# One key-tile sequence for batches three to seven of a sliding-window attention with an MLP behind it

## The chip, the cores and the metric

The kernel runs on one core of a Trainium2 chip. The metric is the device time of one launch in microseconds (us). PE is the matrix engine, ACT the scalar engine, DVE the vector engine, POOL GpSimd, and SP the sync engine, which here only issues DMAs. "L849" is line 849 of the kernel before.

## The reference, cut to what matters

```python
batch, n_heads, seq, head_dim = (8, 8, 576, 64)
window = 32
scores = (q @ k^T) / sqrt(64)
mask = abs(pos[:, None] - pos[None, :]) <= window
attn = softmax(where(mask, scores, -1e9))
x = (attn @ v) -> [4608 tokens, 512]      # 8 batches x 576 tokens, heads side by side
h = x @ w_in                               # w_in 512 x 2048
g = s * relu(h)^2 + b
out = g @ w_out                            # w_out 2048 x 512, float32
```

Each token attends to at most 65 tokens of its own batch and head. The MLP then runs over all 4608 tokens.

## The kernel before, in words

*Attention.* The 576 keys of a batch are cut into 9 tiles of 64 (NTILE). A tile of keys meets a window of 128 queries: its own 64 and 32 on either side. Two neighbouring tiles make a unit, on the two halves of the partitions, so a batch has 5 units (NUNIT), and the fifth has only one tile. A unit is one PE part for the scores (`qk_part`, L594, 64x64 corners of the array), an exponential on ACT (L620), a product with a 0/1 band mask on DVE (L624), a PE part for probabilities times V (`av_part`, L650), and `finish`: a reciprocal and a product on DVE (L670, L672), and then the transpose into XT, the MLP's input. In batches 0 to 2 that transpose is done by PE and copied by ACT (L679, L684), from batch 3 on by a DMA transpose from SP (L690). A unit's output are the 128 rows from 32 ahead of its first key; 96 in the first and the last unit of a batch. The V part of one unit and the score part of the next are issued together (`unit`, `pe_part`, LAG = 1).

*Loads.* q and k of batches 2 and up come in pieces (`piece`): one DMA for 512 rows, a cast to bf16 (L543, in two halves), a DMA transpose from SP (L550), and for k a reordering copy on POOL (L560). V comes by unit (`load_v`) and is cast on DVE (L485). `late(b)` says which engine issues these loads: SP for b < LATE, ACT from there on. Loads are held back by `paced`, which waits for an earlier unit's V part. q, k and V have two slots each, by the parity of the batch.

*MLP.* Tokens are cut into blocks of 96, 128, 288 and eight times 512. `s1` makes one 128-wide slice of h for a block (L849: 4 matmuls), ACT takes the relu (L856), DVE squares it (L858). `s2` sums 16 matmuls for 128 tokens into O (L867), DVE scales and shifts (L880), SP writes out. s1 of a block needs XT of all its tokens: block 4 (tokens 1024 to 1535) needs batch 2's rows.

*Order.* No order of instructions is written by hand. `_Graph` holds tasks with a cost, dependencies and a key (about when it is due); `plan` schedules them as a list, each engine taking the task that can start first, then the smaller key. It also models the two DMA queues (SP, ACT): each transfer has a size and a cost, RING bounds what stands in a queue before the issuing engine has to wait, and ACT only issues when its queue is short (CALM). Each engine then runs its list strictly in order. So a changed cost or key may change the order of anything.

Of the kernel before, what the change touches and what calls it, by code (L numbers as in the profile page):

```python
# [18 lines left out]
NUNIT = (NTILE + 1) // 2  # L19
VW = 66  # L20
# [9 lines left out]
XPE = 3  # L30
PACE = ((-1, -1, -1),) * 3
CASTS = 20.0
LATE = 2
AFTERV = 4
KTV = 0
CASTE = (("pool", "pool"), ("dve", "dve"))
# [24 lines left out]
class _Graph:  # L61
# [6 lines left out]
    RING, CALM, ISSUE, WRITE = 112.0, 40.0, 1400.0, 600.0  # L68
# [37 lines left out]
    def plan(self):  # L106
# [63 lines left out]
        while len(order) < len(self.tasks):  # L170
# [35 lines left out]
            room.clear()  # L206
        self.order = order
# [96 lines left out]
def bass_sliding_window_symmetric__then__act_starrelu_kernel(  # L304
# [22 lines left out]
    with ExitStack() as es:  # L327
# [24 lines left out]
        VB = [sb((128, NUNIT, H, VW), BF16, "vb") for _ in range(2)]  # L352
        EXS = sb((128, NEX, 2, NPAIR, 128), BF16, "ex")
        EX = [EXS[:, i, :, :, :] for i in range(NEX)]
        MASK = sb((128, 128), BF16, "mask")
# [43 lines left out]
        def unit_rows(m):  # L399
            lo = max(0, 128 * m - WIN)  # L400
            return lo, min(S, 128 * m + 128 - WIN)

        def due(b, m):
            tok = b * S + unit_rows(m)[0]
            blk = next(x for x in range(NM) if TBLK[x][0] + TBLK[x][1] > tok)
            f = (tok - TBLK[blk][0]) / TBLK[blk][1]
            before = PH[blk] - PH[blk - 1] if blk > 0 else 4.0
            return PH[blk] - 14.0 - (1.0 - f) * before
# [20 lines left out]
        for p0 in (0, 64):  # L429
            band(MASK[p0:p0 + 64, :], ONESW[p0:p0 + 64, :], ("MASK", p0), 0, 64, -96)  # L430
        for i in range(2):
            for c0 in (0, WIN + S):
                zero("dve", QT[i][:, :, c0:c0 + WIN], ("QTZ", i, c0), 150, key=-98 if i == 0 else -20)
            add("dve", lambda e, i=i: e.memset(VB[i].rearrange("p t h c -> p (t h) c")[:, :, D:D + 1], 1.0), 150,
# [13 lines left out]
        def load_weights(which, i, x, key, eng):  # L448
# [6 lines left out]
            else:  # L455
# [4 lines left out]
                dma=("l", 16, 92.0) if which == "in" else ("l", 32, 50.0))  # L460
# [5 lines left out]
        def paced(b, u):  # L466

            return land["av", b - 1, u] if u >= 0 else land["av", b - 2, NUNIT + u]

# [4 lines left out]
        def load_v(b, t, key, waits=()):  # L474

            n = min(128, S - 128 * t)
            add(late(b),
                lambda e: e.dma_start(VST[0:n, t, :, :], v[b, :, 128 * t:128 * t + n, :].rearrange("h p d -> p h d")),
                650.0, writes=[("VST", t)], key=key, dma=("l", n // 2, 23.0), waits=waits)
            land["v", b, t] = g.tasks[-1]  # L480

        def cast_v(b, t, key, eng, slack):
            slot, n = b % 2, min(128, S - 128 * t)
            add(eng, (lambda e: e.copy(VB[slot][0:n, t, :, 0:D], VST[0:n, t, :, :])) if eng == "act" else
                (lambda e: e.tensor_copy(VB[slot][0:n, t, :, 0:D], VST[0:n, t, :, :])),  # L485
                {"act": 617.0, "dve": 420.0, "pool": 750.0}[eng],
                reads=[("VST", t)], writes=[("V", slot, t)], key=key, slack=slack)

        def load_pair(b, name, pr, key, load_key, banks, eng, slack):
# [6 lines left out]
                600.0, writes=[("STG", si)], key=load_key, dma=("l", 8, 112.0))  # L496
# [26 lines left out]
        def piece(b, parts, key, waits):  # L523
# [16 lines left out]
                dma=("l", sum(n for _, _, n, _ in parts) // 8, 68.0))  # L540
# [26 lines left out]
        def later(b, key):  # L567
# [6 lines left out]
            for i, parts in enumerate(((("q", 0, 512, 0),), (("k", 0, 512, 0),), (("q", 512, 64, 0), ("k", 512, 64, 32)))):  # L574
                piece(b, parts, key + 0.01 * i, [paced(b, PACE[min(b, 4) - 2][i])] +
                      ([land["v", b - 1, AFTERV]] if b > (1 if LATE == 2 else 2) and AFTERV >= 0 else []))
# [8 lines left out]
        def buffers(b, u):  # L585
            n = b * NUNIT + u
            return EX[n % NEX], n % NEX, EX[(n - 1) % NEX], (n - 1) % NEX

        def tiles(u):
            return [j for j in (2 * u, 2 * u + 1) if j < NTILE]  # L590

        def qk_part(b, u, hps=(0, 1)):
            slot = b % 2
            fns = [lambda e, pr=pr, j=j, hp=hp: e.matmul(  # L594
                SC[64 * (j % 2):64 * (j % 2) + 64, hp, pr * 128:pr * 128 + 128],
                lhsT=KT[slot][64 * hp:64 * hp + 64, pr, 64 * j:64 * j + 64],
                rhs=q_window(b, pr, j)[64 * hp:64 * hp + 64], start=True, stop=True)
                for pr in range(NPAIR) for j in tiles(u) for hp in hps]
            lo, hi = max(0, 128 * u - WIN), min(S, 128 * u + 128 + WIN)
            reads = [("QT", slot, x, pr) for x in pieces(lo, hi, 64) for pr in range(NPAIR)]  # L600
            reads += [("KT", slot, x, pr) for x in tiles(u) for pr in range(NPAIR)]
            if u == 0:
                reads.append(("QTZ", slot, 0))
            if u == NUNIT - 1:
                reads.append(("QTZ", slot, WIN + S))
            return fns, reads, [("SC", hp) for hp in hps], 230.0 if len(hps) == 2 or u == NUNIT - 1 else 440.0

        def exp_mask(b, u, hps=((0, 1),)):
            key = due(b, u)
            ex, ei, _, _ = buffers(b, u)  # L610
            n = 64 * len(tiles(u))
            for hs in hps:
                dst, src = ex[0:n, hs[0]:hs[-1] + 1, :, :], SC[0:n, hs[0]:hs[-1] + 1, :].rearrange("p i (a c) -> p i a c", a=NPAIR)
                flat = dst.rearrange("p i a c -> p (i a) c")
                if b > 1:
                    flat_src = src.rearrange("p i a c -> p (i a) c").rearrange("p a (i c) -> p a c i", i=4)
                    flat_dst = flat.rearrange("p a (c i) -> p a c i", i=4)
                else:
# [4 lines left out]
                mask = MASK[0:n, :].rearrange("p (one c) -> p one c", one=1).to_broadcast((n, 4 * len(hs), 128))  # L623
                add("dve", lambda e, flat=flat, mask=mask: e.tensor_tensor(flat, flat, mask, ALU.mult),  # L624
                    130 + 0.53 * 512 * len(hs), reads=[("E", ei, hp, pr) for hp in hs for pr in range(NPAIR)] + [("MASK", p0) for p0 in (0, 64)],
# [6 lines left out]
        def av_part(b, u):  # L632


            slot = b % 2
            ex, ei, px, pi = buffers(b, u)
            bank, res = av_banks(b, u)
# [3 lines left out]
            def put(h, x, g):  # L641
# [3 lines left out]
                if not 0 <= j < NTILE:  # L645
# [7 lines left out]
                    rhs=VB[slot][64 * g:64 * g + 64, j // 2, h, 0:D + 1], start=first, stop=True,  # L653
# [339 lines left out]
```

The softmax here doesn't subtract the row's maximum and nothing guards it: scores larger than these inputs give would overflow.

## Time and profile before

| | |
|---|---|
| time, median of 3 runs | 324.03 us (323.0 to 324.18) |
| span in the profile | 321.4 us |
| PE, ACT, DVE, POOL busy | 295.8, 141.2, 206.6, 66.1 us |
| s1 matmuls (L849) and s2 matmuls (L867) | 139.6 and 139.6 us busy |
| exp of a unit (L620), 35 times | 1.02 us each, with 64 partitions as with 128 |
| mask product (L624), 35 times | 0.76 us each |
| reciprocal, product (L670, L672), 34 times each | 0.20 and 0.69 us each |
| cast of q/k pieces (L543) on DVE, POOL | 0.68, 1.04 to 1.38 us each |

Busy time of PE has overlaps and modelled ends, so idle time is better read from gaps and waits. The first score parts of batches 2, 3 and 4 begin at 80.89, 103.1 and 132.0 us; the last V part begins at 256.7 us. From there to the end there is MLP only.

### The profile page before, as it was taken

To read this page: it belongs to the slowest core of one execution; us is meant where nothing else is said; L and a number is where in the kernel's file an instruction comes from. 1 tells how busy PE (TensorE), PEld (TensorE's weight loads), DVE (VectorE), ACT (ScalarE), POOL (GpSimd) and SP (SyncE) were. 2 spreads that over 40 slices of the span, in tenths; PEclk is the share of its full clock that TensorE was granted. 3 is DMA by queue.
4 is the path that set the end of the run, shared out by engine and by line. 5 is a ranking of instruction groups with operands and counts; after the bars stand their busy time and mean duration, and the time that the engine had idled before them with its cause. 6 is when DMAs were issued, how large, how long until landed. Compare 5 with 4: busy or idle time off the path is not lost.

```text
span 321.4 us, 8084 instructions
## 1 busy us (share of the span) xinstructions
PE 295.8 (92%) x3410; PEld 160.8 (50%) x3452; DVE 206.6 (64%) x402; ACT 141.2 (44%) x219; POOL 66.1 (21%) x78
## 2 busy tenths in 40 slices
PE   2776999999998999999999999999999999999995
PEld 2564787755554444454444444454444444444442
DVE  2764678767869894979477769786965543333311
ACT  3653366445423863455055544553454423333200
POOL 3446454555106000600140006001500000000000
PEclk9999999999999999999999999999999999999999
DMA  7999999897995999789929994999312210000021
GB/s 254 292 284 332 355 209 335 289 230 186 214 234 175 280 151 181 172 244 190 229 90 306 146 223 85 294 187 224 93 49 67 69 60 33 35 33 33 35 98 66
DMA packets 104580, 56.70 MB, mean 176 GB/s; under 512 B 77216, under 2 KB 96160, under 8 KB 104544
## 3 DMA queue, kind: packets, MB, share of 16 engines
q1 hardware_dynamic: 62208, 34.94, 46.0%
q10 hardware_dynamic: 42336, 21.24, 28.8%
q8 instruction: 27, 0.44, 0.7%
q14 instruction: 9, 0.07, 0.1%
HBM read 36.70 MB, written 9.44 MB: 144 GB/s over the span
## 4 chain that ended last, share of the span: by engine, by line
PE 78%; DMA 9%; DVE 5%; issue 3%; ACT 2%; ACTq 1%; SPq 1%; POOL 0%
PE o L867 35%; PE w L849 34%; PE avn L650 4%; DMA stg<-in_moe_w_out_dram 3%; DMA vst<-in_v_dram 3%; DMA stg<-in_moe_w_in_dram 2%; PE sc L594 2%; DVE gt L858 1%; DVE ex L624 1%; PE o L890 1%; DVE xn L672 1%; DVE outs L880 1%; DMA stg<-in_q_dram 1%; PE sc L505 1%; ACT r L856 1%
## 5 line engine op out<-in xcount | busy, mean ns | idle before, releaser
L849 PE MATMUL w<-xt,win 128*128 128x512 bf16 (+3 forms) x679 | 139.6, 341 | 5.5 <-issue 2.8
L867 PE MATMUL o<-wout,gt 128*128 128x512 bf16 (+1 forms) x623 | 139.6, 357 | 5.1 <-DVE wout L462 2.5
L856 ACT ACTIVATE r<-w 128x512 bf16<-128x512 f32 (+2 forms) x152 | 86.8, 575 | 113.0 <-PE w L849 99.1
L858 DVE TENSOR_TENSOR gt<-r 128x512 bf16<-128x512 bf16 (+2 forms) x152 | 75.5, 503 | 67.3 <-ACT r L856 66.7
L867 PEld LDWEIGHTS o<-wout,gt 128*128 128x128 bf16 x640 | 61.0, 98 | 64.6 <-DVE wout L462 2.8
L849 PEld LDWEIGHTS w<-xt,win 128*128 128x128 bf16 x704 | 60.5, 99 | 59.5 <-ACT r L856 2.9
L560 POOL COPY kt<-ktr 128x512 bf16<-128x512 bf16 (+1 forms) x30 | 31.8, 1060 | 128.2 <-DMA ktr<-nat 126.8
L620 ACT ACTIVATE ex<-sc 128x1024 bf16<-128x1024 f32 (+1 forms) x35 | 35.8, 1023 | 30.7 <-PE avn L650 24.1
L880 DVE SCALAR_TENSOR_TENSOR outs<-o,sb,cvec 128x512 f32<-128x512 f32 (+1 forms) x40 | 27.7, 692 | 16.7 <-PE o L867 16.4
L624 DVE TENSOR_TENSOR ex<-ex,mask 128x1024 bf16<-128x1024 bf16 (+1 forms) x35 | 26.6, 760 | 5.5 <-ACT ex L620 4.6
L672 DVE TENSOR_TENSOR xn<-avn,rec 128x512 bf16<-128x512 f32 (+1 forms) x34 | 23.4, 688 | 0.8
L650 PE MATMUL avn<-vb,ex 64*64 64x65 bf16 x976 | 22.0, 199 | 1.9 <-ACT xt L684 1.0
L650 PEld LDWEIGHTS avn<-vb,ex 64*64 64x64 bf16 x976 | 14.3, 108 | 15.9 <-issue 7.2
L485 DVE CAST vb<-vst 128x512 bf16<-128x512 f32 (+1 forms) x32 | 20.1, 632 | 0.0
L543 DVE CAST nat<-stg 128x1024 bf16<-128x1024 f32 (+1 forms) x30 | 19.7, 677 | 0.0
L594 PE MATMUL sc<-qt,kt 64*64 64x128 bf16 x504 | 14.8, 217 | 0.0
L670 DVE RECIPROCAL rec<-avn 128x8 f32<-128x8 f32 (+1 forms) x34 | 6.9, 203 | 7.9 <-PE avn L650 7.6
L505 PE MATMUL w<-ident,nat 64*64 64x64 bf16 x144 | 5.5, 239 | 6.5 <-ACT nat L498 4.5
L462 POOL CAST win<-stg 128x1024 bf16<-128x1024 f32 x8 | 8.3, 1042 | 10.7 <-DMA stg<-in_moe_w_in_dram 10.7
L594 PEld LDWEIGHTS sc<-qt,kt 64*64 64x64 bf16 x504 | 9.8, 107 | 0.6 <-POOL kt L560 0.4
L462 POOL CAST wout<-stg 128x1024 bf16<-128x1024 f32 x6 | 6.6, 1096 | 8.6 <-DMA stg<-in_moe_w_out_dram 8.6
L505 PEld LDWEIGHTS w<-ident,nat 64*64 64x64 bf16 x144 | 4.7, 151 | 7.0 <-ACT nat L498 4.5
(63 smaller groups left out, 101.3 us busy)
## 6 DMA issues: line engine op xcount, KB each, us to landing
out_dram<-outs SPq DMA_DIRECT2D x32, 256.0 KB, 2.3
vst<-in_v_dram ACTq DMA_DIRECT2D x24, 256.0 KB, 5.5
stg<-in_q_dram ACTq DMA_DIRECT2D x6, 1024.0 KB, 5.5
stg<-in_k_dram ACTq DMA_DIRECT2D x6, 1024.0 KB, 8.0
stg<-in_moe_w_in_dram SPq DMA_DIRECT2D x8, 512.0 KB, 7.8
stg<-in_moe_w_out_dram SPq DMA_DIRECT2D x8, 512.0 KB, 9.3
stg<-in_q_dram SPq DMA_DIRECT2D x8, 288.0 KB, 5.8
stg<-in_k_dram SPq DMA_DIRECT2D x8, 288.0 KB, 5.8
```

The costliest lines, as they stand in the source:

```text
L485: (lambda e: e.tensor_copy(VB[slot][0:n, t, :, 0:D], VST[0:n, t, :, :])),
L560: add("pool", lambda e, c=c, w=w: e.tensor_copy(KT[slot][:, :, c:c + w].rearrange("p a (s i) -> p a s i", i=4), KTR[slot][:, :, :, c // 4: ...
L594: fns = [lambda e, pr=pr, j=j, hp=hp: e.matmul(SC[64 * (j % 2):64 * (j % 2) + 64, hp, pr * 128:pr * 128 + 128], lhsT=KT[slot][64 * hp:64 * ...
L620: add("act", lambda e, dst=flat_dst, src=flat_src: e.activation(dst, src, AF.Exp, bias=0.0, scale=0.125), 190 + 0.833 * 512 * len(hs), rea ...
L624: add("dve", lambda e, flat=flat, mask=mask: e.tensor_tensor(flat, flat, mask, ALU.mult), 130 + 0.53 * 512 * len(hs), reads=[("E", ei, hp, ...
L650: return [lambda e: e.matmul(av[64 * x:64 * x + 64, h, 0:D + 1], lhsT=buf[64 * g:64 * g + 64, h % 2, h // 2, c:c + 64], rhs=VB[slot][64 * ...
L672: add("dve", lambda e: e.tensor_tensor(XN[xi][0:p1, :].rearrange("p (a c) -> p a c", a=H), av[0:p1, :, 0:D], REC[ri][0:p1, :].rearrange("p ...
L849: add("pe", [lambda e, g=g, kc=kc: e.matmul(wt[:, g, :], lhsT=WIN_BF[:, kc, (f0 + g) * 128:(f0 + g + 1) * 128], rhs=XT[:, kc, t0 % XR:t0 % ...
L856: add("act", lambda e: e.activation(rt, wt, AF.Relu, bias=0.0, scale=1.0), 190 + 0.833 * ng * nt, reads=[("W", wb)], writes=[("R1", rb)], ...
L858: add("dve", lambda e: e.tensor_tensor(GT[gs][:, f0:f0 + ng, g0:g0 + nt], rt, rt, ALU.mult), 130 + 0.53 * ng * nt, reads=[("R1", rb)], wri ...
L867: add("pe", [lambda e, fc=fc: e.matmul(O[:, ob, 0:cn], lhsT=GT[gs][:, fc, g0:g0 + 128], rhs=WOUT_BF[:, fc, c0:c0 + cn], start=(fc == 0), s ...
L880: add("dve", lambda e: e.scalar_tensor_tensor(OUTS[us][:, 0:cn], O[:, ob, 0:cn], SB128[:, 0:1], CVEC[:, c0:c0 + cn], ALU.mult, ALU.add), 2 ...
```

## The change

From batch 3 on the key tiles of all batches form one sequence: 5 x 9 = 45 tiles, two to a unit, in 23 units where there were 25 (`seq_of`, `seq_tiles`, `tile_at`, `group_of`). Two of these units straddle: one tile is the last of a batch, the other the first of the next. There the window of a tile would look into the neighbouring batch, so four masks take the place of one (`mask_of`): in three of them the 32 columns on the far side of a batch's end are zero in one or both halves. V's casted copy becomes a ring of ten units, and a straddling unit's V comes by two DMAs. A few things come with it:

- LATE goes from 2 to 4: loads of q, k and V of batches 2 and 3 are issued by SP, those from batch 4 on still by ACT.
- CASTE: from batch 3 on one of the two halves of each q/k cast goes to POOL, where both were on DVE. CASTS doubles, so that these casts yield to other work that is ready.
- The planner's costs of several transfers change (w_in 92 to 103, w_out 50 to 48.5, V of batches 0 and 1 23 to 21, pieces from ACT 68 to 61), and after a DMA transpose SP is kept until its queue is down to PUSH.

The diff, cut to its core:

```diff
+LONG = 3
+PAIRS = 2
-XPE = 3
+XPE = 15
-CASTS = 20.0
-LATE = 2
-AFTERV = 4
-CASTE = (("pool", "pool"), ("dve", "dve"))
+CASTS = 40.0
+LATE = 4
+CASTE = (("pool", "pool"), ("pool", "dve"))
...
+            if t.dma[0] == "t":
+                free[t.stream] = max(free[t.stream], space(t.stream, self.PUSH))
...
-        VB = [sb((128, NUNIT, H, VW), BF16, "vb") for _ in range(2)]
+        VB = sb((128, 2 * NUNIT, H, VW), BF16, "vb")
...
-        MASK = sb((128, 128), BF16, "mask")
+        MASKS = [sb((128, 128), BF16, "mask") for _ in range(4)]
...
+        def seq_of(b):
+            return min(b, LONG)
+        def seq_tiles(c):
+            return NTILE * (1 if c < LONG else B - LONG)
+        def tile_at(c, t):
+            return c + t // NTILE, t % NTILE
+        def group_of(b):
+            if b < LONG:
+                return range(NUNIT)
+            u0 = (NTILE * (b - LONG)) // 2
+            return range(u0, (NTILE * (b + 1 - LONG) + (b == B - 1)) // 2)
...
+        for i, cuts in ((1, ((0, 96), (64, 0))), (2, ((64, 96),)), (3, ((0, 0),))):
+            add("pool", lambda e, i=i: e.tensor_copy(MASKS[i][:, :], MASK[:, :]), 250,
+                reads=[("MASK", 0, 0), ("MASK", 0, 64)], writes=[("MASK", i, 0), ("MASK", i, 64)], key=0.0)
+            for p0, c0 in cuts:
+                add("pool", lambda e, i=i, p0=p0, c0=c0: e.memset(MASKS[i][p0:p0 + 64, c0:c0 + WIN], 0.0), 150,
+                    writes=[("MASK", i, p0)], key=0.0)
...
-                dma=("l", 16, 92.0) if which == "in" else ("l", 32, 50.0))
+                dma=("l", 16, 103.0) if which == "in" else ("l", 32, 48.5))
...
-            return land["av", b - 1, u] if u >= 0 else land["av", b - 2, NUNIT + u]
+            c, v = seq_of(b - 1), group_of(b - 1)[0] + u
+            while v < 0:
+                c, v = c - 1, v + NUNIT
+            return land["av", c, v]
...
-                dma=("l", sum(n for _, _, n, _ in parts) // 8, 68.0))
+                dma=("l", sum(n for _, _, n, _ in parts) // 8, 68.0 if late(b) == "sp" else 61.0))
...
-                      ([land["v", b - 1, AFTERV]] if b > (1 if LATE == 2 else 2) and AFTERV >= 0 else []))
+                      ([land["v", seq_of(b - 1), group_of(b - 1)[-1]]] if b > PAIRS or LATE == PAIRS else []))
...
-            for b in range(2, B):
-                later(b, due(b, 0) - 24.0)
-                for t in range(NUNIT):
-                    load_v(b, t, due(b, t) - 35.0, waits=[paced(b, PACEV[min(b, 4) - 2][t])] + ([land["kt", 2, 0]] if b == 2 and KTV else []))
-                    cast_v(b, t, due(b, t) - 4.0, EV2[t], SLACK[3])
-                for u in range(NUNIT):
-                    unit(b, u)
+            for b in range(PAIRS, B):
+                c = seq_of(b)
+                later(b, due(c, group_of(b)[0]) - 24.0)
+                for i, u in enumerate(group_of(b)):
+                    load_v(c, u, due(c, u) - 35.0, late(b), [paced(b, PACEV[min(b, 4) - 2][i])])
+                    cast_v(c, u, due(c, u) - 4.0, EV2[i], SLACK[3])
+                for u in group_of(b):
+                    unit(c, u)
```

XPE counts units now (15 of them in batches 0 to 2), so PE still transposes in the same batches.

## The prediction

> **What bounds the kernel now.** I read the page first, then the busy time by stages, the waits of PE, the chain of waits around the one stage that looked loose, and last the timeline of PE around single units. From the page's first two parts (a slice is 8.03 us; the last line is what DMA moved in each):
>
> ```profile
> PE 295.8 (92%) x3410; PEld 160.8 (50%) x3452; DVE 206.6 (64%) x402; ACT 141.2 (44%) x219; POOL 66.1 (21%) x78
> PE   2776999999998999999999999999999999999995
> GB/s 254 292 284 332 355 209 335 289 230 186 214 234 175 280 151 181 172 244 190 229 90 306 146 223 85 294 187 224 93 49 67 69 60 33 35 33 33 35 98 66
> ```
>
> PE is the bound: 9 tenths in nearly every slice from the sixth on. What PE does not spend on work is 321.4 - 295.8 = 25.6 us. The busy time by stages says where that lies (PE is the first engine column, the columns after it PEld, DVE, ACT, POOL):
>
> ```profile
> 0.00:40.00 40.00, 26.52 (x564) 21.34 (x566) 23.27 (x52) 19.10 (x33) 17.84 (x29) 1.00 0.98 303
> 40.00:80.00 40.00, 39.06 (x603) 27.65 (x599) 30.61 (x57) 21.87 (x37) 20.47 (x23) 1.00 0.96 251
> 80.00:104.00 24.00, 22.06 (x330) 11.98 (x334) 19.85 (x35) 9.22 (x13) 6.72 (x7) 1.00 0.96 210
> 104.00:140.00 36.00, 33.80 (x392) 16.53 (x398) 28.21 (x57) 21.03 (x32) 5.55 (x5) 1.00 1.07 209
> 140.00:250.00 110.00, 106.91 (x1211) 52.72 (x1230) 80.95 (x157) 50.77 (x76) 15.56 (x15) 1.00 0.85 168
> 250.00:321.00 71.00, 67.41 (x329) 30.57 (x333) 23.66 (x47) 19.23 (x32) 0.00 (x0) 1.00 0.13 48
> ```
>
> 13.5 us lie in the first 40 us, where DMA (the column before GB/s) is at 0.98 and the weights arrive. 0.9 lie in 40 to 80, 1.9 in 80 to 104, 2.2 in 104 to 140, 3.1 in 140 to 250. So after the start there are about 8 us of idle at most, and the waits of PE from 80 us on show that few of them are waits for another engine (us in total, times, longest; first answer 80 to 110, second 110 to 250):
>
> ```profile
> PE avn L650 <- ACT xt L684: 1.0, 1, 1.0
> ...
> PE w L849 <- issue: 2.3, 13, 0.4
> PE o L867 <- issue: 1.3, 8, 0.2
> PE avn L650 <- DVE ex L624: 0.7, 1, 0.7
> PE w L849 <- ACT r L856: 0.5, 3, 0.2
> ```
>
> Most of the "issue" rows are gaps of 0.16 us ahead of a group that lists 3 or 11 matmuls where the program has 4 or 12: a missing record, not idle time. What remains as true waits is 1.0, 0.2 for DVE xn in the first answer, 0.7 and 0.5, about 2.4 us.
>
> The price of one attention unit on PE comes from its timeline, at a unit with one key tile (between the first and the last line, with one group of four L849 after it):
>
> ```profile
> 213.22 1.03 PE L867 MATMUL o<-wout,gt 128*128 128x512 bf16 x4
> ...
> 214.33 0.39 PE L594 MATMUL sc<-qt,kt 64*64 64x128 bf16 x8
> ...
> 215.70 1.89 PE L867 MATMUL o<-wout,gt 128*128 128x512 bf16 x8
> ```
>
> The chain spaces full matmuls by 1.73 / 8 = 0.216 us, so a group of four takes 0.864. The group ahead of the unit ends at 213.22 + 0.864 = 214.08, the group behind it begins at 215.70 - 0.864 = 214.84: the one-tile unit costs 0.75 us of PE. The same sum for a two-tile unit (groups of four at 237.04 and at 239.52, with the unit and one group between) gives 239.52 - 0.864 - 237.04 - 0.864 = 0.75. Half a unit costs as much as a whole one.
>
> **What the Trainium skill says.** "TensorEngine Tiling (Array Packing)", section "Key Properties": tiles run independently of each other, and changing the tiling mode drains the array. The trace agrees: 8 score matmuls cost what 16 do, since the other half of the array stands idle, and PE shows some 0.1 us of gap on entering a unit. "DMA: Bandwidth & Descriptors", section "Issuing engines are not separate DMA queues": DMAs issued by different engines run on the same 16 DMA engines, and issuing from another one saves only the sequencer's time. So moving loads from ScalarE to SyncE changes order, not bandwidth. The trace agrees as to size: an issue takes 0.34 to 0.45 us of ACT's queue, 2.29 at worst. "GPSIMD Engine Reference", section "Key points": GpSimd is about twice as slow as VectorE in elementwise work and shares its SBUF interface. Trace: the cast of L543 takes 1.04 us or more on POOL against 0.68 on DVE; what sharing costs no row isolates.
>
> **The change part by part.** (a) *One sequence for batches 3 to 7.* 25 units become 23 (45 tiles, two each): two fewer, because five single-tile units become one. The score matmuls (72 per batch) and output matmuls (144 per batch) are all still there, packed in fewer units; 2 x 0.75 = 1.5 us of PE go. PE is the bound from 40 us to the end, so I count all of it. Beside it go 2 x (1.02 exp) on ACT, 2 x (0.79 + 0.20 + 0.69) = 3.4 us on DVE, and about six transposes of 1.2 us each on SP. These lie beside PE's work and count nothing by themselves.
>
> (b) *The masks.* Three POOL copies of 128x128 and four memsets. The trace has no such copy; nearest from below is a memset of 0.10, from above the qt memset or the affine select at 0.29 to 0.31. 7 x 0.1 to 7 x 0.3 gives 0.7 to 2.1 us; I take 1.5. They are ready at 3.2 us and POOL idles until 6.02 (2.79 us, waiting for q of batch 0), so they are hidden. If the planned order put them behind that cast, batch 0 could start up to 2 us late; I keep this for the upper end.
>
> (c) *Casts.* For batches 3 to 7, three of six casts per batch go to POOL: 15 casts, 10 x 0.68 + 5 x 0.67 = 10 us of DVE away, 15 x about 1.1 = 17 us on POOL, whose busy share after 60 us is low. The larger CASTS makes them yield to all else that is ready. Matters only where DVE's queue holds PE, which is 96 to 103 us. The chain of waits there (start, us, what):
>
> ```profile
> 96.40 0.69 DVE xn L672
> ...
> 97.99 1.55 DVE ex L624
> 99.55 0.67 DVE outs L880
> ```
>
> Here DVE, with V casts of L485 between these lines, leads to the PE wait of 1.0 at 103.04. From 85 us to 103.67, when the matmuls of block 4 (L849) begin, PE lives on L867 groups and attention alone; by then these have run out. Block 4 needs batch 2's rows, so this is the one stage where attention's latency sets PE's time.
>
> (d) *Loads of batches 2 and 3 on SP.* This decides when batch 2 is ready. Before: w_out's last four loads leave SP from 44.49 to 47.28, q of batch 2 leaves ACT at 50.6 and k at 55.9 (8.0 us to landing, 64), POOL casts run from 61.54 after 2.77 us behind a memset that waits for batch 1, kt copies from 75.85, first scores at 80.89. After: q and k of batch 2 need only stage buffers freed at about 42 us and stand behind w_out on one queue, issued at 48 or so. w_out's 2.1 MB and q, k of 2.4 MB at the 335 GB/s of the slice 48 to 56 take 13.4 us, so k lands at about 44.5 + 13.4 = 58: an estimate, 6 us sooner. Casts then run from 56 to 61 and first scores come at about 76, some 5 us sooner. So PE's wait at 103 and the small ones next to it (1.0 + 0.2) go. Against this: SP is in order. Behind a full queue stand out_dram writes (five OUTS buffers, so DVE can go on through four more before it waits, and PE's O banks behind it) and batch 2's own transposes, on which kt and so PE's scores wait. I take half a microsecond for such waits on PE, between 0 and the 6 us of rival 2.
>
> (e) *Straddling units* need the next batch's first tile, so rows 480 to 575 of batches 3 and 5 (and the last 32 of 4 and 6) close with the next batch. Their loads leave at the same PE part as before (the pace counts back one unit), so the cycle from batch to batch is unchanged, and PE has MLP work at all these times: nothing. The two extra V issues (0.4 us each on ACT) likewise. The wait of 0.7 at 136.86 (DVE ex, behind a V cast) probably goes with DVE lighter by (a) and (c): 0.5.
>
> Sum: 1.5 + 1.2 + 0.5 - 0.5 = 2.7 us off 324.03: 321.3.
>
> **The rivals.** (1) Units only: the waits at 103 and 137 come back elsewhere in the new order. 324.0 - 1.5 = 322.5, on the border of what can be told. For it: true waits are only 2.4 us in all, and any new order has some. (2) Slower: batch 3's q and k (2.1 MB, 6 us at 335 GB/s) get ahead of batch 2's transposes on SP, or batch 2's loads get stuck behind out writes. Then block 4 starts late, and as the fillers had run out, PE waits one for one: 324.0 - 1.5 + 4 = 326.5, 329 at worst. For it: SP already waits 84 us for outs in all. Against: the planner knows this queue. (3) The start gains: 13.5 us of idle there, and the new DMA costs reorder casts and matmuls among the weights. PE's wait of 2.5 for a wout cast is the largest piece that an order could fill: 321.3 - 2 = 319.3. Against: loads keep their order there, and arrivals bind. A loss of 1 is as possible.
>
> **How the numbers follow.** My forecast 0.55, rival (1) 0.15, (2) 0.17, (3) 0.13. Within 0.5% is 322.4 to 325.65. Faster: 0.49 of the first, 0.07 of (1), 0.13 of (3): 0.69. Same: 0.06 + 0.08 + 0.02 = 0.16. Slower: 0.15 from (2). The range goes from 318.4 (below it only the best of (3)) to 326.0, which leaves out the worse half of (2) and bad mask placement.
>
> **What would show it.** Right: 33 exp groups of L620's successor instead of 35, two fewer reciprocals, AV and score matmul counts unchanged; batch 2's first scores near 76 us; no PE wait above 0.5 us at the start of block 4; PE busy about 1.5 us less. Wrong: first scores of batch 2 after 81 us, out_dram waits on DVE, PE idle above 2 us between 80 and 110, or a first 40 us with more than 13.5 us idle.

## The result, and the profile after

The changed kernel takes 318.93 us (median of 4 runs, 318.43 to 320.56) where the kernel before takes 323.88 (4 runs, 323.0 to 324.18). The ratio is 0.986, with a 95% interval of 0.982 to 0.9901. A run that takes over 1.5% longer than the fastest of its kernel on its chip is called slow, and medians and ratios below leave slow runs out. In the profiles the span goes from 321.4 to 316.5 us, 4.9 less; the prediction said 2.7 less.

The lines have new numbers: s1 is L920 (was L849), s2 L938 (L867), scores L651 (L594), probabilities times V L709 (L650), exp L679 (L620), the kt copy L617 (L560), the q/k casts L600 (L543), the transpose into XT by DMA L753 (L690). From the page's first part, to set against that of before:

```profile
PE 294.2 (93%) x3413; PEld 160.6 (51%) x3452; DVE 192.7 (61%) x379; ACT 139.3 (44%) x217; POOL 86.5 (27%) x100
```

PE's busy time fell by 1.6 us, its idle time from 25.6 to 316.5 - 294.2 = 22.3. So about 1.6 us are work that is gone and 3.3 are waiting that is gone. About, because 3452 weight loads go with only 3410 and 3413 recorded matmuls: a missing record counts as idle time of PE. The run with the old casts (below), whose span is the same as here (316.6 us), has all 3452 matmuls, and its PE is busy 298.8 us. So some 4 us of what looks idle in these two profiles are missing records, about as many in both. DVE is lighter by 13.9 us and POOL heavier by 20.4. Busy time by stages of the kernel after (after the stretch's length: PE, PEld, DVE, ACT, POOL busy with counts, PE clock, DMA share, GB/s):

```profile
0.00:40.00 40.00, 28.05 (x576) 22.43 (x577) 23.14 (x53) 19.87 (x34) 19.34 (x36) 1.00 0.96 302
40.00:80.00 40.00, 37.96 (x597) 27.15 (x596) 28.47 (x57) 21.41 (x36) 21.35 (x24) 1.00 0.97 233
80.00:104.00 24.00, 23.20 (x326) 12.73 (x330) 17.20 (x31) 11.77 (x17) 9.06 (x8) 1.00 0.97 223
104.00:140.00 36.00, 35.00 (x424) 17.34 (x427) 26.93 (x56) 19.18 (x30) 10.81 (x9) 1.00 1.05 226
140.00:250.00 110.00, 107.29 (x1196) 52.56 (x1214) 75.39 (x144) 50.30 (x75) 25.95 (x23) 1.00 0.91 168
250.00:316.50 66.50, 62.71 (x308) 28.43 (x312) 21.54 (x43) 16.79 (x29) 0.00 (x0) 1.00 0.13 49
```

PE's idle time is the length less its busy time. Stage by stage, before and after:

| stage, us | idle before | idle after | gone |
|---|---|---|---|
| 0 to 80 | 13.48 + 0.94 | 11.95 + 2.04 | 0.43 |
| 80 to 104 | 1.94 | 0.80 | 1.14 |
| 104 to 140 | 2.20 | 1.00 | 1.20 |
| 140 to 250 | 3.09 | 2.71 | 0.38 |
| 250 to the end | 3.59 + 0.4 not in the view | 3.79 | 0.2 |

With the 1.6 us of work this is the 4.9. The 0.38 is mostly no waiting: from 140 to 250 us there are 18 gaps of 0.16 us before and 16 after, each ahead of a group that lacks a matmul. About two thirds of the waiting that went lay between 80 and 140 us, where batches 2 and 3 are prepared and blocks 4 and 5 of the MLP begin. The waits of PE that are left there (us in total, times, longest; first answer 80 to 104, second 104 to 250):

```profile
PE o L938 <- issue: 0.5, 3, 0.2
PE w L920 <- ACT r L927: 0.3, 2, 0.2
...
PE w L920 <- issue: 2.1, 13, 0.2
PE o L938 <- issue: 1.0, 6, 0.2
PE w L920 <- ACT r L927: 0.5, 3, 0.2
```

None is over 0.2 us, and the relu rows (ACT r), like the issue rows, are gaps of 0.16 us ahead of groups that lack a matmul. The rows of before with 1.0 (ACT xt), 0.7 (DVE ex) and 0.4 (issue) are gone.

**Was it the start?** PE's idle time in the first 40 us fell by 1.5 us, which looks like rival (3), but from 40 to 80 it rose by 1.1. A better test is to ask where both kernels stand at one moment, here 66 us. Matmul records can be missing, but the weight loads are complete (3452 in both), one to a matmul. Those of s1 and s2 from 66 us to the end, before:

```profile
66.00:321.40 255.40, 120.78 (x483) 47.31 (x504) 1.00 0.70 147
...
66.00:321.40 255.40, 128.29 (x539) 53.32 (x556) 1.00 0.70 147
```

and after (the second count in each row is that of the weight loads):

```profile
66.00:316.50 250.50, 121.30 (x486) 48.00 (x510) 1.00 0.72 151
...
66.00:316.50 250.50, 127.67 (x531) 52.37 (x544) 1.00 0.72 151
```

At 0.216 us for a 512-wide matmul and half of it for the 256-wide ones (44 and 32 of s2's, all beyond 512), MLP work of 504 x 0.216 + 512 x 0.216 + 44 x 0.108 = 224.2 us is left before, and 510 x 0.216 + 512 x 0.216 + 32 x 0.108 = 224.2 after. The V parts have 864 weight loads left in both. At 66 us the two kernels stand at the same place, to within a matmul or two, and so all of the 4.9 us comes later, to a few tenths: what is not MLP falls from 255.4 - 224.2 = 31.2 us to 250.5 - 224.2 = 26.3. The two units that are gone are 1.5 of it, and 3.4 remain for waits. In this pair of profiles the start decided nothing.

**The largest waits that went.** The first is the one that the prediction named, ahead of block 4. PE's timeline before:

```profile
101.67 0.40 PE L679 MATMUL avn<-ident,xn 128*128 128x128 bf16 x4 [0.17 <-DVE xn L672]
103.04 0.26 PE L650 MATMUL avn<-vb,ex 64*64 64x65 bf16 x7 [0.97 <-ACT xt L684]
```

The transposes of batch 2 (L679) are followed at once by the V part that waits for ACT's copy of them. PE's timeline after, at batch 2's first scores and the starts of blocks 4 and 5:

```profile
76.34 0.42 PE L651 MATMUL sc<-qt,kt 64*64 64x128 bf16 x16
...
97.02 1.89 PE L938 MATMUL o<-wout,gt 128*128 128x512 bf16 x8
98.75 1.89 PE L920 MATMUL w<-xt,win 128*128 128x512 bf16 x8
...
120.90 4.48 PE L938 MATMUL o<-wout,gt 128*128 128x512 bf16 x19
125.22 1.89 PE L920 MATMUL w<-xt,win 128*128 128x512 bf16 x8
```

Batch 2's scores come at 76.34 instead of 80.89, and block 4 begins at 98.75 instead of 103.67, directly behind an s2 group. The next was not named. PE's timeline before, at the start of block 5:

```profile
125.19 1.03 PE L867 MATMUL o<-wout,gt 128*128 128x512 bf16 x4
126.64 1.89 PE L849 MATMUL w<-xt,win 128*128 128x512 bf16 x8 [0.43 <-issue]
```

The group of four ends at 125.19 + 0.864 = 126.05, so PE stood still for 0.59 us. The group behind the gap lists all its eight matmuls, so no record is missing. The profile puts the gap at 0.43, as it counts from a modelled end of the matmul before. Block 4's 64 matmuls of s1 have run by 126.05; this is the first group of block 5, which needs the first 320 rows of batch 3. These come by DMA transposes from SP. In the program the last rows of them leave with the second of the three xt transposes before, and with the second of the two after. SP's queue before, with the landing of that second transpose (line L690, 119.6 to 120.8 us):

```profile
111.60 6.63 SPq L550 DMA_TRANSPOSE qt<-nat  x1
118.28 3.93 SPq L690 DMA_TRANSPOSE xt<-xn  x3
...
DMA to landing us min/median/max: 7.0/7.0/7.0
```

and after (line L753, 118.93 to 120.1 us):

```profile
111.01 6.55 SPq L607 DMA_TRANSPOSE qt<-nat  x1
117.61 2.56 SPq L753 DMA_TRANSPOSE xt<-xn  x2
...
DMA to landing us min/median/max: 4.0/4.0/4.0
```

Before, the second transpose goes out at 119.6 us and lands 7.0 later, at 126.6, where block 5 begins (126.64). After, it goes out at 118.9 and lands at 122.9, ahead of the start of block 5 at 125.22, which has no gap. No row names the transpose as the releaser; the program's order and its landing within 0.1 us of block 5's start speak for it. A q transpose holds SP's queue for over 6.5 us in front of it in both kernels, so that is not the difference. Most of the difference is the time to landing, 3.0 us less, and why that is shorter is not shown. With the wait of 0.69 for DVE at 136.86 the profile's rows give 0.43 + 0.69 = 1.12 us in the stage that lost 1.20.

### The profile page after: what moved, and what is told of

Its sections match the earlier page's. It is cut to its first block, busy times and chain, and to the rows that moved or that the text cites. A ratio compares the mean times of both kernels' runs of the same rounds, so it can differ in the third digit from the quotient of the medians.

```text
span 316.5 us, 8094 instructions
## 1 busy us (share of the span) xinstructions
PE 294.2 (93%) x3413; PEld 160.6 (51%) x3452; DVE 192.7 (61%) x379; ACT 139.3 (44%) x217; POOL 86.5 (27%) x100
## 4 chain that ended last, share of the span: by engine, by line
PE 78%; issue 2%; ACT 1%; DVE 1%
PE o L938 37%; PE w L920 35%; PE avn L709 4%; PE sc L651 2%; PE o L961 1%; ACT r L927 1%; PE avn L740 0%; DVE ex L683 0%; ACT ex L679 0%; DVE outs L951 0%; PE w L709 0%; PE w L740 0%
## 5 line engine op out<-in xcount | busy, mean ns | idle before, releaser
L920 PE MATMUL w<-xt,win 128*128 128x512 bf16 (+3 forms) x678 | 138.9, 341 | 4.9 <-issue 2.4
L938 PE MATMUL o<-wout,gt 128*128 128x512 bf16 (+1 forms) x627 | 140.2, 357 | 2.6 <-issue 1.4
L929 DVE TENSOR_TENSOR gt<-r 128x512 bf16<-128x512 bf16 (+2 forms) x152 | 77.8, 518 | 72.5 <-ACT r L927 71.7
L938 PEld LDWEIGHTS o<-wout,gt 128*128 128x128 bf16 x640 | 61.1, 98 | 62.4 <-DVE wout L508 0.9
L920 PEld LDWEIGHTS w<-xt,win 128*128 128x128 bf16 x704 | 61.0, 99 | 58.8 <-POOL win L508 1.0
L617 POOL COPY kt<-ktr 128x512 bf16<-128x512 bf16 (+1 forms) x30 | 32.6, 1086 | 55.5 <-DMA ktr<-nat 54.0
L679 ACT ACTIVATE ex<-sc 128x1024 bf16<-128x1024 f32 (+1 forms) x33 | 33.8, 1023 | 22.3 <-PE avn L709 20.5
L600 POOL CAST nat<-stg 128x1024 bf16<-128x1024 f32 (+1 forms) x21 | 24.8, 1183 | 57.2 <-DMA stg<-in_q_dram 23.3
L683 DVE TENSOR_TENSOR ex<-ex,mask 128x1024 bf16<-128x1024 bf16 (+1 forms) x33 | 23.7, 717 | 1.8 <-ACT ex L679 0.5
L733 DVE TENSOR_TENSOR xn<-avn,rec 128x512 bf16<-128x512 f32 (+1 forms) x32 | 22.1, 689 | 0.9
L709 PE MATMUL avn<-vb,ex 64*64 64x65 bf16 x976 | 20.8, 199 | 0.6 <-DVE ex L683 0.4
L709 PEld LDWEIGHTS avn<-vb,ex 64*64 64x64 bf16 x976 | 13.5, 108 | 13.9 <-issue 7.0
L542 DVE CAST vb<-vst 128x512 bf16<-128x512 f32 (+1 forms) x30 | 15.1, 502 | 0.7 <-DMA vst<-in_v_dram 0.7
L651 PE MATMUL sc<-qt,kt 64*64 64x128 bf16 x504 | 13.4, 216 | 0.0
L600 DVE CAST nat<-stg 128x1024 bf16<-128x1024 f32 (+1 forms) x15 | 11.1, 738 | 1.3 <-DMA stg<-in_k_dram 1.3
L651 PEld LDWEIGHTS sc<-qt,kt 64*64 64x64 bf16 x504 | 8.8, 107 | 0.6 <-POOL kt L617 0.4
```

The lines of the kernel that those rows point to most:

```text
L600: add(eng, lambda e, x=x: e.tensor_copy(nat[0:top, 1024 * x:1024 * x + 1024].rearrange("p (i h d) -> p h i d", h=H, i=2), stg[0:top, :].re ...
L617: add("pool", lambda e, c=c, w=w: e.tensor_copy(KT[slot][:, :, c:c + w].rearrange("p a (s i) -> p a s i", i=4), KTR[slot][:, :, :, c // 4: ...
L651: fns = [lambda e, pr=pr, x=x, b=b, j=j, hp=hp: e.matmul(SC[64 * x:64 * x + 64, hp, pr * 128:pr * 128 + 128], lhsT=KT[b % 2][64 * hp:64 * ...
L679: add("act", lambda e, dst=flat_dst, src=flat_src: e.activation(dst, src, AF.Exp, bias=0.0, scale=0.125), 190 + 0.833 * 512 * len(hs), rea ...
L709: return [lambda e: e.matmul(av[64 * x:64 * x + 64, h, 0:D + 1], lhsT=buf[64 * g:64 * g + 64, h % 2, h // 2, c:c + 64], rhs=VB[64 * g:64 * ...
L733: add("dve", lambda e: e.tensor_tensor(XN[xi][0:p1, :].rearrange("p (a c) -> p a c", a=H), av[0:p1, :, 0:D], REC[ri][0:p1, :].rearrange("p ...
```

## The experiments

Times are compared with runs of the kernel before on the same chip, or with another kernel on the same chip, since the kernel before took 323.9 us beside the changed kernel above and 325.7 to 327.3 in the later runs. The changed kernel itself has two more sets of runs:

> The changed kernel itself again, on the chip of the next three. In the runs so far the kernel before took 327.25 us on one chip and 323.88 on another, so parts of the change are compared with this one. Theory: the kernel with the old casts is the changed kernel as far as time goes (its time from 66 us to the end that is not MLP matmuls was 26.4 us, as here 26.3), so this one lies within 0.5% of it as a ratio to the kernel before, near 0.98 on that chip, near 0.986 on the first. Rival: the casts cost or gained over 1 us.

> The changed kernel as the anchor of the next three on their chip. Ratio to the kernel before 0.983 to 0.986 as in its two runs; from 66 us to the end its time that is not MLP matmuls 26.1 to 26.3 us, which is what 28 units at 0.75 us, five PE transposes of 0.22 and an end of 3.7 us add up to, so no idle time that an order could still take away after 66 us.

**Measured:** 320.35 us against 325.74 before, ratio 0.9829 (0.9787 to 0.9871); and 321.22 against 326.07, 0.9858 (0.9797 to 0.9919). The gain is 4.9 to 5.4 us on these chips. In the profile of the second set the time from 66 us on that is not MLP matmuls is 27.8 us, not the 26.1 to 26.3 expected, with a wait of 0.50 for DVE at 68.65: the same kernel does not wait the same in every execution.

**Without the sequence.** Every batch has five units again, all else as in the changed kernel (the second line only keeps the branch for an odd tile from an empty sequence):

```diff
-LONG = 3
+LONG = 8
...
-            if seq_tiles(LONG) % 2 == 0:
+            if LONG < B and seq_tiles(LONG) % 2 == 0:
```

> The changed kernel with the batches kept apart again (five units each, 25 instead of 23 in batches 3 to 7); loads, casts and the planner's costs stay as changed. Theory 1 (a unit costs PE 0.75 us, and PE is the bound): PE busy up by 1.5 to 1.6 us, time up by 1.5 us against the changed kernel, to about 320.4. Rival (the gain is all in the waits, the spared units were hidden): time within 0.5 us of 318.9.

> The kernel without the sequence once more, now beside the changed one. Theory 1 (two units less on PE and nothing else): 1.5 us, ratio to the changed kernel 1.005. Rival (the sequence also takes away waits of PE or ACT work at the batch ends): from 104 us to the end its time that is not MLP matmuls is 2.6 us more than the changed kernel's as in the first run, time up by 2.5 us or more.

**Measured:** 324.09 us (ratio to before 0.9902, 0.9863 to 0.9941), and beside the changed kernel's 320.35 on one chip 323.78 (0.9941, 0.9915 to 0.9967). PE is busy 296.7 us in the second, 294.6 in the changed kernel beside it, with as many matmuls recorded. So the sequence is worth about 3.5 us within the changed kernel, not 1.5. What the other 2 are is seen in PE's timeline of the second. From 60 us on it has these four waits over 0.2 us; the changed kernel beside it has none:

```profile
62.75 1.05 PE L938 MATMUL o<-wout,gt 128*128 128x256 bf16 x8 [1.30 <-issue]
...
108.22 1.67 PE L920 MATMUL w<-xt,win 128*128 128x512 bf16 x7 [0.16 <-ACT r L927]
...
156.57 1.04 PE L920 MATMUL w<-xt,win 128*128 128x512 bf16 x4 [0.79 <-ACT r L927]
...
158.75 1.90 PE L938 MATMUL o<-wout,gt 128*128 128x512 bf16 x7 [0.29 <-DVE gt L929]
...
190.64 0.25 PE L709 MATMUL avn<-vb,ex 64*64 64x65 bf16 x6 [0.34 <-POOL kt L617]
```

The line at 108.22 is one of ten with 0.16 for the relu: each stands ahead of a group of 7 where the program has 8, so they are missing records and no waits. The four come to 2.7 us; with 1.5 for the units 4.2, where the spans differ by 4.7 (321.4 and 316.7). The wait for the relu (ACT r) at 156.57 comes from ACT's queue. ACT's timeline in this run, and then the same place in the first run of the same kernel:

```profile
153.23 2.59 ACTq L533 DMA_DIRECT2D vst<-in_v_dram  x1
155.92 1.09 ACT L927 ACTIVATE r<-w 128x512 bf16<-128x512 f32 x2 [2.10 <-PE w L920]
```

```profile
153.91 0.60 ACTq L533 DMA_DIRECT2D vst<-in_v_dram  x1
```

An issue of a V load held ACT for 2.59 us, and the relu behind it started only then. "DMA: Bandwidth & Descriptors", section "Issuing engines are not separate DMA queues", in the Trainium skill calls the time to initiate a DMA usually small relative to the DMA; this trace shows one of 2.59 us, with 6.9 us to its landing, on an engine that PE waits for. But in the first run the same issue took 0.60 us, and no relu wait over 0.2 us is seen there; of the four waits only the issue gap (0.94 at 63.45) and the one for gt (0.29 at 158.47) come again. So this wait is one of the execution and not of the kernel alone.

That suggests a theory: the rest is loads on ACT, which collide with the relu. In two runs all loads go to SP, once without and once with the sequence:

```diff
-LATE = 4
+LATE = 8
```

> The kernel without the sequence, with all loads on SyncE (LATE at 8). Taking the sequence away cost 3.6 us where two units are worth 1.5; in that kernel a V load held ScalarE's queue 2.59 us at 153 us, and PE waited 0.8 us for the relu behind it. Theory (the rest of the 3.6 us are waits of that kind, which come and go with the order and with loads on ScalarE, and not the sequence itself): time 1 to 2 us under the kernel without the sequence, so 1.5 to 2.5 us over the changed kernel. Rival (the rest is bound to the extra units): 3.6 us over the changed kernel again.

> The changed kernel with all loads on SyncE (LATE at 8). Theory (the changed kernel has no such wait left, though a load holds ScalarE's queue 3.2 us at 149 us): time within 0.5 us of the changed kernel, or slower by 1 us if transposes and loads on one queue hold each other up. Rival (loads on ScalarE still cost): faster by 0.5 us or more, and then a version better than both.

**Measured:** without the sequence 325.62 us, 0.9979 (0.9949 to 1.0009); with it 322.93, 0.9893 (0.9836 to 0.9951), on the chip on which the changed kernel took 321.22. Taking all loads off ACT helped neither. The first is 4.4 us over the changed kernel, where the theory has 1.5 to 2.5, so loads on ACT cause such a wait at times, but the theory falls as an explanation of the other 2 us. That these are bound to the extra units, as the rival has it, fits the number and is not shown by it. With the sequence and without, the kernels are 2.7 us apart here: most of what the sequence is worth doesn't hang on where the loads are issued.

**The sequence alone.** LATE, the casts and the planner's costs as before:

```diff
-CASTS = 40.0
-LATE = 4
-CASTE = (("pool", "pool"), ("pool", "dve"))
+CASTS = 20.0
+LATE = 2
+CASTE = (("pool", "pool"), ("dve", "dve"))
...
-            if t.dma[0] == "t":
-                free[t.stream] = max(free[t.stream], space(t.stream, self.PUSH))
...
-                dma=("l", 16, 103.0) if which == "in" else ("l", 32, 48.5))
+                dma=("l", 16, 92.0) if which == "in" else ("l", 32, 50.0))
```

(and in the same way the costs of V and of the q/k pieces)

> The sequence alone on the kernel before: LATE at 2, casts and planner's costs of before. Theory 1 (the sequence is worth 1.5 us wherever it stands): 1.5 us under the kernel before. Theory 2 (2.5 us as above): 2.5 us under. Rival (the early loads or the costs are needed for it): time as before, within 0.5 us. First scores of batch 2 stay at about 81 us in all three.

**Measured:** 323.07 us, 0.9928 (0.9905 to 0.9952): 2.3 to 2.7 us of gain, half of the whole and near theory 2. The first scores of batch 2 come at 85.15 us, not at 81; in this profile PE's clock dips for some 6 us before 40 us (last section). The wait ahead of block 4 is still there (timeline of PE; L707 is probabilities times V here):

```profile
107.39 0.26 PE L707 MATMUL avn<-vb,ex 64*64 64x65 bf16 x7 [0.97 <-ACT xt L743]
```

So the sequence alone doesn't remove that wait.

**The loads.** Issue of batches 2 and 3 back on ACT in the changed kernel, and to SP in the kernel before:

```diff
-LATE = 4
+LATE = 2
```

> The changed kernel with LATE at 2: loads of batches 2 and 3 issued by ScalarE again, as before the change. Theory 1 (loads on SyncE make batch 2 ready some 5 us sooner, and that took away the stall where block 4 begins): first scores of batch 2 back at about 81 us instead of 76, a PE wait of about 1 us before the first s1 matmuls of block 4, time up by 1 to 1.5 us, to about 320.2. Rival (DVE, lightened by the casts and spared units, took the stall away, not the queue): no such wait, time within 0.5 us of 318.9.

```diff
-LATE = 2
+LATE = 4
```

> The kernel before with LATE at 4 alone. Theory 1 (the prediction's step on loads): first scores of batch 2 at about 76 us, the PE wait of 1.0 us at 103 us gone, time 1 to 1.5 us under the kernel before. Rival (an earlier batch 2 is not worth anything by itself; the gain in the changed kernel comes from the whole new order): first scores at 76 us, but other waits in place of the one at 103, time within 0.5 us of the kernel before.

**Measured:** the first takes 322.38 us, 0.9867 (0.9822 to 0.9911), 2.2 us more than the changed kernel with its old casts on the same chip (320.20, below). Batch 2's first scores go back to 80.93 us, as expected, but the loss isn't where it was expected. Block 4 starts with no gap, since an s2 group stands between batch 2's transposes and the V part, and PE runs out later instead, around the start of batch 4's attention (timeline of PE):

```profile
102.23 0.39 PE L740 MATMUL avn<-ident,xn 128*128 128x128 bf16 x4
102.46 1.89 PE L938 MATMUL o<-wout,gt 128*128 128x512 bf16 x8
...
104.91 1.90 PE L920 MATMUL w<-xt,win 128*128 128x512 bf16 x8
...
127.02 3.78 PE L938 MATMUL o<-wout,gt 128*128 128x512 bf16 x16 [0.28 <-DVE gt L929]
131.88 0.32 PE L709 MATMUL avn<-vb,ex 64*64 64x65 bf16 x16 [1.08 <-POOL kt L617]
```

So the wait ahead of block 4 can go without an early batch 2. The casts and the planner's costs, which this run has and the sequence alone has not, must bear on it; which of them does it no run separates.

The second takes 324.50 us against 326.07, 0.9956 (0.9928 to 0.9983): 1.4 to 1.6 us of gain. Its timeline of PE:

```profile
77.56 0.42 PE L594 MATMUL sc<-qt,kt 64*64 64x128 bf16 x16
...
80.61 1.05 PE L867 MATMUL o<-wout,gt 128*128 128x256 bf16 x8 [0.81 <-DVE outs L880]
...
104.27 1.90 PE L849 MATMUL w<-xt,win 128*128 128x512 bf16 x8
...
127.76 1.90 PE L867 MATMUL o<-wout,gt 128*128 128x512 bf16 x8 [1.15 <-DVE gt L858]
```

Scores come 3.3 us sooner and the wait of 1.0 at 103 is gone, but others, of 0.81 and 1.15 and one of 0.78 with no releaser at 147.11, take its place: rival (1) at work. From 60 us on the waits over 0.2 us come to 2.74 us here and to 2.09 in the profile of the kernel before. So where the gain comes from is not seen in these profiles, and that it is near the 1.2 us of the prediction's step is no proof of that step. Moving these loads brings batch 2 forward in any case; whether this is kept depends on the order around it.

**The casts.** The old halves and the old cost:

```diff
-CASTS = 40.0
+CASTS = 20.0
...
-CASTE = (("pool", "pool"), ("pool", "dve"))
+CASTE = (("pool", "pool"), ("dve", "dve"))
```

> The changed kernel with both halves of the q and k casts of batches 3 to 7 on VectorE and CASTS at 20, as before the change. Theory 1 (VectorE's queue held PE at about 137 us and partly at 97 to 103 us): VectorE busy up by 10 us, a PE wait of 0.5 to 1 us between 80 and 140 us comes back, time up by 0.5 us. Rival (VectorE has room once batch 2 is early): busy up by 10 us, time within 0.3 us of 318.9.

**Measured:** 320.20 us, 0.9793 (0.9753 to 0.9834) to before, a span of 316.6. DVE is busy 201.1 us instead of 192.7, the span is that of the changed kernel (316.5 and 316.7), and from 60 us on PE has no wait over 0.2 us: the casts bring nothing. DVE was not the bound where they were moved.

**The planner's costs.** The old costs of transfers, and no hold of SP after a transpose (the diff is that of the sequence alone, without its first three lines):

> The changed kernel with the planner's transfer costs of before (w_in 92, w_out 50, V 23, pieces 68, pairs 112, nothing after a DMA transpose). Theory 1 (the costs reorder the matmuls among the arriving weights, and PE no longer stands 2.5 us before the first w_out): PE idle in the first 40 us back at about 13.5 us from 12.0, the 2.5 us wait for the w_out cast back, time up by 1 to 1.5 us. Rival (what the start gained was given back by 80 us, idle 2.0 instead of 0.9 there, so it is worth 0.4): time up by under 0.5 us.

**Measured:** 320.58 us, 0.9799 (0.9751 to 0.9846), 0.4 more than the run with the old casts beside it, which is less than the intervals tell apart. Its profile doesn't look like theory 1: in the first 40 us PE is idle 12.9 us, and the wait for the first w_out cast is 0.6, not 2.5. But it has waits of 0.91 for DVE outs at 80.06, 0.29 for gt and 1.18 for kt at 162.81, more than the median of its runs lets one expect.

**One batch more in the sequence.** Batch 2 joins it (54 tiles, 27 units for batches 2 to 7 instead of 28):

```diff
-LONG = 3
+LONG = 2
```

> The changed kernel with batch 2 in the sequence as well (LONG at 2, 54 tiles, 27 score units where there are 28, and a last part for 32 rows). Theory: half a unit to one unit of PE less, 0.4 to 0.75 us, but the last rows of batch 2 now wait for batch 3's first tile; block 4 needs only batch 2's first 384 rows, so that costs nothing: time 0.3 to 0.8 us under the changed kernel. Rival: batch 3's loads, which are paced by batch 2's units, start later and PE runs dry before block 5: slower by 1 us or more.

**Measured:** 324.29 us, 0.9948 (0.992 to 0.9975), 3.9 us slower than the changed kernel on that chip, though it has one unit less. Its timeline of PE:

```profile
103.94 0.32 PE L709 MATMUL avn<-vb,ex 64*64 64x65 bf16 x16 [1.01 <-ACT xt L745]
...
130.77 0.32 PE L709 MATMUL avn<-vb,ex 64*64 64x65 bf16 x16 [1.32 <-POOL kt L617]
...
151.05 1.90 PE L920 MATMUL w<-xt,win 128*128 128x512 bf16 x8 [0.79 <-ACT r L927]
```

These three alone are 3.1 us. The wait ahead of block 4 is back (1.01); the last is again a relu behind a V load that held ACT's queue for 3.44 us, from 146.85. The rival's size came true, but not its place: ahead of block 5 PE waits no more than 0.28 us. A unit less doesn't pay for an order that puts such waits back. None of the versions is shown to be faster than the changed kernel: those with the old casts and with the old costs have ratios a little lower (0.9793 and 0.9799 against 0.9829 to 0.986), and the intervals overlap.

## Why the prediction was right

The direction was right, and so were the removed work and the two waits that it named; 318.93 lies within the range, and the gain was undersized by 2.2 us. The lower end of the range, 318.4, was there for rival (3), a faster start, which is not what happened: that the time lies within it is in part luck. By the steps of the prediction:

- *(a) Two units less.* Right: 33 exp groups instead of 35, V and score weight loads unchanged in number (976 and 504 in the largest groups), PE busy 1.6 us less for 1.5 predicted. That the units count in full is borne out: without the sequence the time is up by no less than 1.5 us, in the changed kernel and in the kernel before.
- *(b) The masks.* Right. On POOL (timeline, last memset) they take 0.65 + 0.47 + 0.50 + 0.12 = 1.74 us, 1.5 predicted, and end at 5.22, ahead of the cast at 6.12:

```profile
5.10 0.12 POOL L475 MEMSET mask<- 64x32 bf16 x1
6.12 0.66 POOL L556 CAST nat<-stg 128x576 bf16<-128x576 f32 x1 [0.91 <-DMA stg<-in_q_dram]
```

- *(c) The casts.* 10 us were to leave DVE and some of the 0.5 for the wait at 136.86 was put down to them. They do leave it (8.4 us: 201.1 and 192.7 busy), but with the old casts the span is the same and the wait does not come back: they earn nothing. One cast takes 1.18 us on POOL and 0.74 on DVE (means of the page), 1.6 times as long, less than the factor of two that the prediction quotes.
- *(d) The loads on SP.* Right in time; the size came out, the reason only in part. Batch 2's q and k leave SP from 46.98 and 48.08 us ("48 or so"), the first scores come at 76.34 ("about 76"), and the stage from 80 to 104 lost 1.14 us of idle time for 1.2 predicted. But with these loads back on ACT that wait stays away, and the loads alone take it away and put others in its place. That an early batch 2 is enough to clear block 4's start is shown; that it is needed in the changed kernel is not so.
- *(e) Straddling units.* Nothing, as said: no wait of PE over 0.2 us from 80 us on.
- *Rival (2)*, slower, had batch 2's loads or transposes stuck on SP's queue. Its waits for the out writes fell instead (SP for DVE outs, 84.2 us before, 67.7 after). *Rival (3)*, the start, is ruled out for this pair of profiles by the equal state of both kernels at 66 us. *Rival (1)*, waits coming back elsewhere, is not what happened here, but it is what happened with the loads moved in either kernel, with batch 2 in the sequence and with the old costs.

The term that was mis-sized is that of the waits. It was 1.2 + 0.5 - 0.5 = 1.2 us net; 3.4 went, from 66 us on. Taken from start to start, as for block 5 above, the wait ahead of block 4 was 1.4 us for the 1.2 predicted: the s2 group of 100.69 ends at 101.34, block 4 begins at 103.67, and transposes (0.22) and a unit (0.75) lie between. The wait at 136.86 was 0.7 for 0.5. The 0.59 ahead of block 5 was in no step: it had been read with the other "issue" rows as a missing record, although it was the one row of 0.43 among rows of 0.16 and stood ahead of a complete group. The 0.5 set aside for new waits measured next to nothing. So 2.7 of the 3.4 are placed, and with the 1.5 for the units 4.2 of the 4.9. Of the other 0.7, 0.24 lie ahead of a complete group at 180.98 and 0.2 behind 250 us (the table); the rest is not placed. The opposite slip was in the prediction's sum of true waits: its 0.5 for the relu are three rows of 0.16 ahead of groups of 7 (at 117.64, 141.93 and 182.82), so these were missing records.

Why the order of the changed kernel is so free of waits stays open. The parts alone bring 2.3 to 2.7 us (the sequence) and 1.4 to 1.6 (the loads); taken out of the whole they cost about 3.5 and 2.2. That each is worth more in the presence of the other is what these medians suggest; the intervals are too wide to show it. The casts alone, the costs alone and the hold of SP after a transpose were not run in the kernel before. What the runs show is which waits come back (relu, kt, gt, xt), in places that differ from version to version, and for one and the same kernel from run to run: over 0.2 us and from 60 us on, 0.35, 0 and 0.50 us in three profiles of the changed kernel, 1.2 and 2.7 in two of that without the sequence. Each version here has one or two profiles, so a single wait in one of them explains the time of that execution, not the median. Loads on ACT are not the one rule behind these waits.

## What to carry to other kernels

Where a planner writes the order, count a change's removed work first (here 1.5 us of the 4.9), and give the waits a range as wide as all the true waits of the profile, since a change of order can clear nearly all of them or bring as many back. Before calling an idle row a missing record, look whether the group behind it is complete and whether its length stands out from its neighbours; one such row ended where a transpose landed. Compare busy times only between profiles with as many records. To learn whether a start matters, compare what is left to do at one moment of both traces, by records that are complete, rather than the idle time of the first slices.

## What the runs showed of the hardware that was not expected

**The TensorE clock dips once in many runs.** In eight of the twelve experiments' profiles the granted clock falls to about half, between 26 and 40 us, for 3 to 4 us in most and some 6 in one (the sequence alone). The same changed kernel had spans of 316.5 and 316.7 us without it and 320.2 with it (on another chip). Busy time of the latter in that stretch (PE clock is the third value from the right):

```profile
34.00:36.00 2.00, 2.00 (x13) 1.32 (x14) 1.00 (x4) 0.41 (x1) 1.04 (x1) 0.75 1.10 367
36.00:38.00 2.00, 2.00 (x14) 1.40 (x13) 0.91 (x2) 0.50 (x2) 0.21 (x1) 0.50 1.06 387
38.00:40.00 2.00, 2.00 (x35) 1.93 (x33) 0.98 (x2) 1.02 (x3) 1.49 (x2) 0.90 1.04 367
```

In the profile of the changed kernel above the same three slices have a clock of 1.00 and 27 to 49 matmuls. Every run has a mean clock. The profiles with a dip have 0.989 to 0.995, those without 0.999 or 1.0; if one below 0.998 is counted as a dip, 80 of 105 runs of the kernel before and 9 of 16 of the changed kernel have it. On one chip (6 runs of the changed kernel, 52 of the one before) runs with it take 325.94 (before) and 320.89 us (changed), runs without it 324.86 and 319.57, so 1.1 to 1.3 us less. On the other chip the kernel before takes 326.40 with it (29 runs) and 324.30 without (8). On the first chip the gain is 5.1 and 5.3 either way, so the dip isn't the cause of the gain. In the Trainium skill, "TensorE: Matmul & The Clock Gate", section "Part 1: The HAM clock gate", says that the array's clock is halved after an idle window of some 3.4 us, that the windows run freely, and that the loss varies from run to run. The depth here agrees with that (0.50), and so does the variation from run to run. The trigger doesn't: the dip of this run came behind a PE wait of 2.04 us for w_out, shorter than such a window, while the run with the old casts waited 2.86 us there without a dip. What sets the dip off is open.

**Arrival of weights varies.** That wait for w_out near 32 us was 0.6, 1.4 and 2.0 us in three profiles of the same changed kernel. A difference of 1 to 2 us in the first 40 us of two single profiles says nothing of the change.
